# Pooled v summed by GpSimd in all units; batch 0's maxima of v later, and its scale moved to the split of x

## The chip, the cores and the metric

The kernel runs on one core of one Trainium2 chip. The metric is the device time of one execution in microseconds (us). The engines of the core are TensorE (PE, its weight loads PEld), VectorE (DVE), ScalarE (ACT), GpSimd (POOL) and SyncE (SP), which issues all the loads and stores here.

## What is computed

An attention over 8 batches, 8 heads, 576 positions of 64 values, and behind it a gated layer.

```python
q_d = q.reshape(B, H, S // 4, 4, D).mean(axis=3)          # k_d, v_d likewise
out_d = softmax(scale * q_d @ k_d.T) @ v_d                # pooled attention
out_up = np.repeat(out_d, 4, axis=2)
scores = np.where(abs(i - j) < 4, scale * q @ k.T, -1e9)  # local attention
x = out_up + softmax(scores) @ v                          # then (4608, 512)
out = (1 / (1 + exp(-(x @ w_gate))) * (x @ w_val)) @ w_out
```

The gated layer is 512 to 1536 to 512 wide. All inputs are of 32 bits; the products of the layer run as three products of 16-bit halves.

## The kernel before

**Units.** The attention is cut into 32 units: unit u is batch u // 4 and a pair of heads u % 4. Units 0 to 3 are batch 0. A unit's steps are made by unit_steps: prep1 copies q into a block tile; prep2 sums q and k over four positions (sum4, line 383); s0 and s1 are the local scores (tile s, then t), with the row maximum, whose subtraction is GpSimd's; sm sums and scales t; vd (vdsum, line 499) sums v over four positions into vdblk, of which there are two; d0 and d1 are the pooled scores (tile sd), their row maxima mxd and exponentials; dn normalizes them; a0 and a1 transpose t (tile at); v copies v into a block tile; at transposes the pooled weights (tile adt); od (av_down) is the pooled product; x (av_local, xsplit) is the local product, its sum with od in xs, and the split of xs in two 16-bit halves in the tile xT, which the gated layer reads.

**sum4.** Two adds: the first, of 384 or 576 columns, is always GpSimd's; the second (line 387) is GpSimd's too, but for vd it is VectorE's in units 0, 1, 2, 3, 6, 9 and 10 (the list vd). It has two instructions of 64x192, one for each half of the partitions.

**Scales.** Each batch has a scale from the largest |v| of its four units: vmax (line 297) reduces one unit's v on VectorE; in a batch's last unit it takes the maximum over the partitions (max_all, line 121: a transpose on TensorE into the tile mxt, a reduction, a second product) and makes pvb, svb and sxb. sxb is read in batch 0 by the eviction of od (line 568) and by the sum xs (line 584).

**Weights.** They come in 36 tiles of 512 KB, each loaded twice into a ring of five buffers (stage): once for its maximum (hmx, line 154, in max_all for tiles 0 to 3 of gate and value, then for the rest), once for the conversion (wconv, line 201), which has three VectorE instructions a tile and a split. The conversion may overwrite the room that batch 0's inputs lie in, so it begins behind batch 0.

**Banks and order.** The results of TensorE lie in eight banks; two of them (ps_a, "att") serve the local scores, the transposes at and the transposes of the maxima, and the rest serve one name each ("gate", "val", "o0" to "o3"). The tile t has two buffers.

**Order.** Each step is entered with a position (function add), and the steps are traced in the order of positions: batch 0's unit u has its base at 1 + 2.36 u, and a step's offset from the list a_... is multiplied by 0.76. Positions are priorities, not times: a planner at compile time (schedule_with_timeline_sim) draws each engine's queue from them and from its own durations; the engines then work through these queues in order, and a step waits for its data and its buffer. Between the units' steps stand products without use ("awake") in batch 0. From position 56 on (C1) the gated layer of chunks 1 to 8, of 512 rows each, sets the pace, and the units of later batches are placed between its products. Chunk 0 runs beside the conversion of the weights.

Of the kernel before, what the change touches and what calls it, by code (L numbers as in the profile page):

```python
# [12 lines left out]
AF = mybir.ActivationFunctionType  # L13
# [3 lines left out]

T = dict(ma=4.5, mas=0.45, mb=9.5, mbs=0.5, c1=56, gs=2.66, g0=16.84, r1=1.99, rs=1.6, ob=3.16, v0=15.13, v1=16.62, v2=17.5, vs=2.12, o0=18, os=1.2, pro=2.36, u4=13.82, u5=21, u6=27, u7=32, l4=1.3, l5=2.77, l6=9.47, l7=8.68, lv=15.08, vm=1.58, b8=6.75, s8=6.63, b12=26.05, s12=8.17, hold=32.07, al=0.76, am=1, z=3.68, sd=0, sn=0.79, v0m=0.61, xd=[2, 3, 7], ad=[0, 3, 7], aa=[0, 1, 2, 3, 6], td=[0, 3, 9, 10], vd=[0, 1, 2, 3, 6, 9, 10], a_prep1=-2.43, a_prep2=-0.89, a_s0=0.01, a_s1=0.52, a_sm=1.82, a_d0=2.39, a_d1=2.6, a_dn=5.17, a_a0=4.37, a_vd=1.97, a_a1=5.1, a_v=2.74, a_at=5.22, a_od=5.79, a_x=8.38, m_prep0=-3.14, m_prep1=-1.14, m_prep2=-1.43, m_s0=0.69, m_s1=2.59, m_sm=3.12, m_d0=2.84, m_d1=5.8, m_a0=10, m_dn=10.78, m_vd=11.67, m_a1=12, m_v=13.07, m_at=13.44, m_od=15.64, m_x=17, k0=30, k_prep1=4, k_prep2=0, k_s0=2, k_s1=2, k_sm=4, k_d0=3, k_d1=0, k_dn=0, k_a0=3, k_vd=8, k_a1=2, k_v=5, k_at=0, k_od=0, k_x=0)  # L20
P = 128
B, H, S, D = 8, 8, 576, 64
NT = B * S
# [1 line left out]
NPAIR = H // 2  # L25
# [5 lines left out]
SD = S // 4  # L31
# [15 lines left out]
NPLAIN = 8  # L47
# [11 lines left out]
def attention_moe(ctx, tc, qk, qkd, v, vd, wg, wv, wo, mask, out):  # L59
    nc = tc.nc  # L60
# [12 lines left out]
    def awake(n):  # L73
        pt = ps_o.tile([P, 512], F32, tag="val", name="awake")
        for i in range(n):
            nc.tensor.matmul(pt[:, :256], idle[:, :P], idle, start=True, stop=True)

    awake(T["k0"])
    ident = cp.tile([P, P], F32, tag="ident", name="ident")
# [19 lines left out]
    def zeroed(eng, shape, dtype, name):  # L99
        t = cp.tile(shape, dtype, tag=name, name=name)  # L100
        eng.memset(t, 0.0)
        return t
# [10 lines left out]
    ad = zeroed(nc.gpsimd, [QM, 2, NKC, 2, WIN], F32, "ad")  # L113
# [27 lines left out]
    def pow2(dst, src):  # L141

        got = max_all(src, src.shape[1])
        nc.vector.tensor_scalar(out=dst, in0=got, scalar1=TINY, scalar2=None, op0=ALU.max)
        nc.vector.tensor_scalar(
            out=dst.bitcast(I32), in0=dst.bitcast(I32), scalar1=EXPBITS, scalar2=None,
            op0=ALU.bitwise_and)
# [5 lines left out]
    def absmax(dst, src):  # L153
        nc.vector.tensor_reduce(dst, src, axis=AX.X, op=ALU.max, apply_absolute_value=True)  # L154

    def split(hi, lo, src, sc):

        nc.scalar.activation(hi, src, AF.Copy, scale=sc)  # L158
        nc.vector.scalar_tensor_tensor(out=lo, in0=src, scalar=sc, in1=hi, op0=ALU.mult, op1=ALU.subtract)  # L159
# [13 lines left out]
    gs = cp.tile([P, NPC], F32, tag="gs", name="gs")  # L173
# [104 lines left out]
    sxb = cp.tile([P, B], F32, tag="sxb", name="sxb")  # L278
# [16 lines left out]
    vm = {}  # L295

    def vmax(u):
        b, hp = divmod(u, NPAIR)
        if hp == 0:
            vm[b] = wk.tile([P, NPAIR], F32, tag="vm", name=f"vm{b}")  # L300
        absmax(vm[b][:, hp : hp + 1], vraw[u].rearrange("p a b -> p (a b)"))
        if hp == NPAIR - 1:
            m1 = wk.tile([P, 1], F32, tag="vm1", name=f"vm1_{b}")
            nc.vector.tensor_reduce(m1, vm[b], axis=AX.X, op=ALU.max)
            pow2(pvb[:, b : b + 1], m1)
            inv_scaled(svb[:, b : b + 1], pvb[:, b : b + 1], 2.0)
            nc.vector.tensor_scalar(out=sxb[:, b : b + 1], in0=svb[:, b : b + 1], scalar1=4096.0, scalar2=None, op0=ALU.mult)
# [96 lines left out]
    def mine(t, u):  # L404
        assert owner[id(t)] == u, (owner[id(t)], u)
# [7 lines left out]
    def unit_steps(u):  # L413
        b, hp = divmod(u, NPAIR)
        s = st[u] = {}
        NQ = 2 * NJ * R
        plain = u < NPLAIN
# [66 lines left out]
        def p2b():  # L484
# [4 lines left out]
            nc.vector.reciprocal(sm, sm)  # L489
            eng = nc.vector if u in T["td"] else nc.gpsimd  # L490
            eng.tensor_tensor(out=t, in0=t, in1=sm.unsqueeze(2).to_broadcast([P, NBLK, WIN]), op=ALU.mult)  # L491
# [7 lines left out]
        def vdsum():  # L499
            take(VDB)  # L500
            x = vdraw[u].rearrange("p a b f -> p (a b) f")
            sum4([(ps, VDB[ps, :, ps], slice(None)) for ps in HALVES], x, nc.vector if u in T["vd"] else nc.gpsimd)

# [15 lines left out]
        def norm_down():  # L519
# [3 lines left out]
            nc.vector.reciprocal(sme, sme)  # L523
            eng = nc.vector if u in T["ad"] else nc.gpsimd
            for qb in range(2):
                if u in T["aa"]:
                    for h in range(2):
# [34 lines left out]
        def av_down():  # L562
            mine(VDB, u)
            pt = bank("o3", f"od_{u}")
            for c in range(NKC):
                product(pt[:, :SD], [VDB[:, c]], [s["adt"][:, c]], c == 0, c == NKC - 1)
            od = wk.tile([P, SD], F32, tag="od", name=f"od16_{u}")
            nc.scalar.activation(od, pt[:, :SD], AF.Copy, scale=sxb[:, b : b + 1])
            s["od"] = od

        def av_local(i0, i1):
            mine(VT, u)
            pt = bank("gate" if i0 == 0 else "val", f"x_{u}_{i0}")
            for i in range(i0, i1):
                product(pt[:, (i - i0) * R : (i - i0 + 1) * R], [x[:, i] for x in VBp], [x[:, i] for x in s["at"]])
            if i0 == 0:
                s["xs"] = wk.tile([P, S], F32, tag="xs", name=f"xs_{u}", bufs=1)
            t0, t1 = i0 * R, min(i1 * R, S)
            g0, g1 = t0 // 4, t1 // 4
            o = s["xs"][:, t0:t1].rearrange("p (g f) -> p g f", f=4)  # L580
            x = pt[:, : t1 - t0].rearrange("p (g f) -> p g f", f=4)
            y = s["od"][:, g0:g1].unsqueeze(2).to_broadcast([P, g1 - g0, 4])
            if plain:
                nc.vector.scalar_tensor_tensor(out=o, in0=x, scalar=sxb[:, b : b + 1], in1=y, op0=ALU.mult, op1=ALU.add)
            else:
                nc.vector.tensor_tensor(out=o, in0=x, in1=y, op=ALU.add)

        def xsplit():
            for c, o, i, n in segs_of_batch(b):
                x = xtile(c)  # L590
                src = s["xs"][:, i : i + n]
                nc.scalar.copy(x[:, hp, 0, o : o + n], src)  # L592
                eng = nc.vector if u in T["xd"] else nc.gpsimd
                eng.tensor_tensor(out=x[:, hp, 1, o : o + n], in0=src, in1=x[:, hp, 0, o : o + n], op=ALU.subtract)  # L594
            del st[u]
            done.add(u)
# [4 lines left out]
            vd=vdsum, v=plain_v if plain else vsplit,  # L601
            a0=lambda: t_local(0, 3), a1=lambda: t_local(3, 5), at=t_down, od=av_down,
            x=lambda: (av_local(0, 8), av_local(8, 10), xsplit()),
# [68 lines left out]
    def add(pos, f):  # L672
        steps.setdefault(pos, []).append(f)
# [45 lines left out]
    for u in range(NU):  # L719
        b, hp = divmod(u, NPAIR)  # L720
        p0 = base(u)
        for k in ALONE if b == 0 else AMONG:
            add(p0 + offset(u, k), units[u][k])
            if b == 0 and T["k_" + k] and k in ("s0", "s1", "d0", "d1", "a0", "a1", "at", "od", "x"):
                add(p0 + offset(u, k), lambda n=T["k_" + k]: awake(n))
        if b == 0:
            if u == 0:
                add(-10, first_loads)
            add(2 + T["v0m"] * hp, lambda u=u: vmax(u))
            continue  # L730
        if b == 1:
            pl = p0 + offset(u, "prep0") - T[f"l{u}"]
            add(max(pl, base(u - 2) + offset(u - 2, "s1") + 0.1) if u > NPAIR + 1 else pl, lambda u=u: load_qk(u))
            add(T["lv"] + 0.2 * hp, lambda u=u: vload(u))
            after = base(u - 1) + 0.1 if u > NPAIR else 0
            add(max(pl + 0.5, after + offset(u - 1, "prep2") if after else 0), lambda u=u: load_qkd(u))
            add(max(pl + 0.5, after + offset(u - 1, "vd") if after else 0), lambda u=u: load_vd(u))
            add(T["lv"] + T["vm"] * (hp + 1), lambda u=u: vmax(u))
            continue
        add(base(u - 2) - 1 if b > 2 else max(base(u - 2) - 1, T["hold"]), lambda u=u: load_qk(u))  # L740
        add(base(u - 1) - 1 if u > 2 * NPAIR else T["hold"], lambda u=u: load_qkd(u))
        add(base(u - 1) + offset(u - 1, "vd"), lambda u=u: load_vd(u))
        pb = base(b * NPAIR)
        add(pb - 5 + hp, lambda u=u: vload(u))
        add(pb + hp, lambda u=u: vmax(u))
# [116 lines left out]
```

## Time and profile before

| | us |
|---|---|
| median of 3 runs | 1129.31 (1126.57 to 1129.5) |
| profiled execution | 1126.46 |
| its span, first to last instruction | 1124.7 |
| TensorE busy | 1079.2 |
| VectorE busy | 567.7 |
| ScalarE busy | 486.7 |
| GpSimd busy | 356.7 |

The mean granted clock of TensorE is 0.972 of its higher level. The profile is that of one execution: its views give each engine's busy time in a stretch, the chain of work that ended last (followed back from the end, at each step to what released it), the instructions of one engine in order of time with the idle time in front of them, and the instructions of one line or one tile with their durations. A "timeline" row that says x2 stands for two instructions that follow each other.

### The profile page before, as it was taken

What the parts mean: (1) busy time and instruction counts of PE and PEld (TensorE: products, weight loads), DVE (VectorE), ACT (ScalarE), POOL (GpSimd) and SP (SyncE); (2) the same over time, 40 slices, a digit from 0 to 9 for tenths busy, and PEclk for the clock granted to TensorE, in tenths of its full rate; (3) what the DMA queues carried; (4) which work ended last, traced back from release to release, by engine and by line L of the source; (5) the groups of instructions that cost most, each with busy time, mean ns of one, the idle gap of its engine ahead of it and who ended that gap; (6) DMA issues with size and microseconds to landing.
All of it is one profiled execution on the core that took longest, in us unless ns stands there. A gap on an engine that the chain in (4) does not pass through costs nothing.

```text
span 1124.7 us, 15921 instructions
## 1 busy us (share of the span) xinstructions
PE 1079.2 (96%) x6191; PEld 592.0 (53%) x6191; DVE 567.7 (50%) x1050; ACT 486.7 (43%) x1112; POOL 356.7 (32%) x416
## 2 busy tenths in 40 slices
PE   7868878999999999999999999999999999999998
PEld 5753434565555555555555555555555554444443
DVE  7779999854445544444444553544444432112121
ACT  6635666544444444454445443544354332222112
POOL 7435646323323433343333332433243210000000
PEclk8759999999999999999999999999999999999999
DMA  9887766432213222132223121322030000000001
GB/s 368 309 293 276 269 224 197 142 108 80 70 48 126 65 67 70 63 114 71 69 69 108 59 69 56 121 70 66 28 117 14 1 1 38 1 1 38 1 1 38
DMA packets 31899, 110.31 MB, mean 98 GB/s; under 512 B 3536, under 2 KB 3664, under 8 KB 31824
## 3 DMA queue, kind: packets, MB, share of 16 engines
q1 hardware_dynamic: 31824, 109.30, 28.2%
q8 instruction: 49, 0.80, 0.3%
q14 instruction: 26, 0.21, 0.1%
HBM read 99.84 MB, written 9.44 MB: 97 GB/s over the span
## 4 chain that ended last, share of the span: by engine, by line
PE 85%; DVE 8%; ACT 2%; DMA 2%; issue 2%; POOL 1%; DVEq 0%; POOLq 0%; SPq 0%; ACTq 0%
PE po L396 24%; PE pg L396 23%; PE pv L396 23%; PE s L396 5%; PE x L396 3%; PE sd L396 2%; PE od L396 2%; PE at L547 1%; PE adt L557 1%; DVE vdblk L387 1%; DVE hmx L154 1%; DVE wrg L210 1%; DMA wg6c<-in_wg_dram 1%; DVE wrv L209 0%; DVE wrg L209 0%
## 5 line engine op out<-in xcount | busy, mean ns | idle before, releaser
L396 PE MATMUL pg<-xT,wg 128*128 128x512 f16 x1296 | 309.8, 382 | 7.5 <-ACT wg L216 4.3
L396 PE MATMUL pv<-xT,wv 128*128 128x512 f16 x1296 | 310.1, 379 | 3.8 <-DVE tanh L628 3.2
L396 PE MATMUL po<-g,wo 128*128 128x512 f16 x1188 | 280.7, 379 | 0.0
L396 PEld LDWEIGHTS <-wg 128*128 128x128 f16 x1296 | 126.8, 99 | 158.1 <-ACT wg L216 6.9
L396 PEld LDWEIGHTS <-wo 128*128 128x128 f16 x1296 | 126.0, 99 | 149.5 <-ACT wo L158 7.4
L396 PEld LDWEIGHTS <-wv 128*128 128x128 f16 x1296 | 125.5, 98 | 144.0 <-issue 3.1
L628 DVE SCALAR_TENSOR_TENSOR tanh<-tanh,pv 128x512 f32<-128x512 f32 x108 | 73.8, 683 | 195.3 <-PE pv L396 187.6
L620 ACT ACTIVATE tanh<-pg,tsc 128x512 f32<-128x512 f32 (+7 forms) x192 | 86.8, 497 | 153.8 <-PE pg L396 153.3
L636 ACT ACTIVATE g<-tanh,gs 128x512 f16<-128x512 f32 x99 | 71.4, 721 | 149.6 <-DVE tanh L628 148.4
L637 DVE SCALAR_TENSOR_TENSOR g<-tanh,gs,g 128x512 f16<-128x512 f32 x99 | 89.1, 900 | 56.7 <-ACT g L636 56.3
L481 POOL TENSOR_TENSOR t<-t,mx 128x640 f32<-128x640 f32 x32 | 43.9, 1372 | 190.3 <-DVE mx L480 190.3
L396 PEld LDWEIGHTS s<-qk,qblk 128*128 128x128 f32 x600 | 77.0, 196 | 12.3 <-DVE t L469 2.1
L396 PE MATMUL s<-qk,qblk 128*128 128x64 f32 x600 | 76.0, 276 | 4.3 <-DVE t L469 1.5
L594 POOL TENSOR_TENSOR xT<-xs,xT 128x384 f16<-128x384 f32 (+7 forms) x58 | 53.1, 931 | 61.0 <-ACT xT L592 60.2
L491 POOL TENSOR_TENSOR t<-t,sm 128x640 f32<-128x640 f32 x28 | 36.1, 1288 | 89.8 <-DVE sm L489 88.6
L487 DVE TENSOR_REDUCE sm<-t 128x10 f32<-128x640 f32 x32 | 26.1, 817 | 58.3 <-ACT t L482 58.3
L158 ACT ACTIVATE vblk<-v,svb 64x640 f16<-64x640 f32 x48 | 39.6, 825 | 35.4 <-PE x L396 34.0
L440 ACT COPY qblk<-qk 64x580 f32<-64x580 f32 x60 | 40.5, 675 | 24.4 <-DMA qk<-in_qk_dram 17.8
L469 DVE SCALAR_TENSOR_TENSOR t<-s,mk 128x384 f32<-128x384 f32 x64 | 31.1, 486 | 37.6 <-PE s L396 37.4
L513 ACT ACTIVATE mxd<-mxd 72x2 f32<-72x2 f32 x64 | 12.9, 202 | 83.7 <-DVE mxd L512 83.0
L159 DVE SCALAR_TENSOR_TENSOR vblk<-v,svb,vblk 64x640 f16<-64x640 f32 x48 | 46.8, 975 | 4.5 <-ACT vblk L158 2.6
L515 ACT ACTIVATE e<-sd,mxd 72x144 f32<-72x144 f32 x128 | 47.0, 370 | 2.4
(296 smaller groups left out, 1177.7 us busy)
## 6 DMA issues: line engine op xcount, KB each, us to landing
qk<-in_qk_dram SPq DMA_DIRECT2D x30, 610.0 KB, 4.0
qkd<-in_qkd_dram SPq DMA_DIRECT2D x29, 576.0 KB, 3.7
vd<-in_vd_dram SPq DMA_DIRECT2D x29, 384.0 KB, 3.5
v<-in_v_dram SPq DMA_DIRECT2D x32, 320.0 KB, 2.9
out_dram<-osb SPq DMA_DIRECT2D x16, 512.0 KB, 2.9
wo<-in_qk_dram SPq DMA_DIRECT2D x2, 610.0 KB, 9.9
wo<-in_qkd_dram SPq DMA_DIRECT2D x2, 576.0 KB, 9.0
out_dram<-osb SPq DMA_DIRECT2D x4, 256.0 KB, 2.3
```

The costliest lines, as they stand in the source:

```text
L158: nc.scalar.activation(hi, src, AF.Copy, scale=sc)
L159: nc.vector.scalar_tensor_tensor(out=lo, in0=src, scalar=sc, in1=hi, op0=ALU.mult, op1=ALU.subtract)
L396: nc.tensor.matmul(o, w[a], x[c], start=first and i == 0, stop=last and i == len(pairs) - 1)
L440: nc.scalar.copy(QB[ps, :, ps.start : ps.start + R], q_[ps])
L481: nc.gpsimd.tensor_tensor(out=t, in0=t, in1=mx.unsqueeze(2).to_broadcast([P, NBLK, WIN]), op=ALU.subtract)
L491: eng.tensor_tensor(out=t, in0=t, in1=sm.unsqueeze(2).to_broadcast([P, NBLK, WIN]), op=ALU.mult)
L515: nc.scalar.activation(s["e"][:, qb, h, :], pt[:QM, h * SD : (h + 1) * SD], AF.Exp, bias=mx[:, h : h + 1], scale=QKSCALE / 16, accum_out=s ...
L594: eng.tensor_tensor(out=x[:, hp, 1, o : o + n], in0=src, in1=x[:, hp, 0, o : o + n], op=ALU.subtract)
L620: nc.scalar.activation(t[:, o : o + n], pt[:, o : o + n], AF.Tanh, scale=tsc[:, b, fc : fc + 1])
L628: nc.vector.scalar_tensor_tensor(out=t, in0=t, scalar=1.0, in1=pt, op0=ALU.add, op1=ALU.mult)
L636: nc.scalar.activation(g[:, 0], t, AF.Copy, scale=gs[:, fc : fc + 1])
L637: nc.vector.scalar_tensor_tensor(out=g[:, 1], in0=t, scalar=gs[:, fc : fc + 1], in1=g[:, 0], op0=ALU.mult, op1=ALU.subtract)
```

## The change

It does four things.

- The list vd is empty: the second add of the pooled v is GpSimd's in all units. In batch 0 the step vd moves from offset 1.97 to 2.6, so behind d0 (2.39) and, at the same position, behind d1 (2.6).
- vmax of batch 0's units stands at 5.5 + 0.3 for each unit in place of 2 + 0.61 for each.
- In batch 0 od is evicted without the scale, and xs is a plain sum.
- In batch 0 the split of x applies the scale: ScalarE makes the high half of scale times xs, and VectorE the low half in one operation of three operands (split, line 156). Before, a copy made the high half and a subtraction the low one: on GpSimd in units 0 and 1, on VectorE in units 2 and 3 (the list xd).

```diff
-T = dict(..., v0m=0.61, ..., vd=[0, 1, 2, 3, 6, 9, 10], ..., a_vd=1.97, ...)
+T = dict(..., v0m=0.61, ..., vd=[], ..., a_vd=2.6, ...)
...
             od = wk.tile([P, SD], F32, tag="od", name=f"od16_{u}")
-            nc.scalar.activation(od, pt[:, :SD], AF.Copy, scale=sxb[:, b : b + 1])
+            if u < NPAIR:
+                nc.scalar.copy(od, pt[:, :SD])
+            else:
+                nc.scalar.activation(od, pt[:, :SD], AF.Copy, scale=sxb[:, b : b + 1])
...
-            if plain:
+            if NPAIR <= u < NPLAIN:
                 nc.vector.scalar_tensor_tensor(out=o, in0=x, scalar=sxb[:, b : b + 1], in1=y, op0=ALU.mult, op1=ALU.add)
             else:
                 nc.vector.tensor_tensor(out=o, in0=x, in1=y, op=ALU.add)
...
                 src = s["xs"][:, i : i + n]
+                if u < NPAIR:
+                    split(x[:, hp, 0, o : o + n], x[:, hp, 1, o : o + n], src, sxb[:, b : b + 1])
+                    continue
                 nc.scalar.copy(x[:, hp, 0, o : o + n], src)
...
-            add(2 + T["v0m"] * hp, lambda u=u: vmax(u))
+            add(5.5 + 0.3 * hp, lambda u=u: vmax(u))
```

## Rows read from the trace of the kernel before

**Rows 1.** The page, busy time of TensorE: us, share of the span, instructions.
```profile
PE 1079.2 (96%) x6191; PEld 592.0 (53%) x6191; DVE 567.7 (50%) x1050; ACT 486.7 (43%) x1112; POOL 356.7 (32%) x416
```

**Rows 2.** Busy time by stretch: length, engines' us (instructions), granted clock, DMA share, GB/s.
```profile
20.00:40.00 20.00, 14.43 (x68) 12.79 (x68) 14.20 (x34) 11.24 (x39) 8.52 (x11) 0.62 1.03 407
...
60.00:80.00 20.00, 13.78 (x60) 12.30 (x59) 14.24 (x29) 4.49 (x10) 3.77 (x7) 0.50 0.79 278
...
160.00:200.00 40.00, 31.39 (x148) 16.28 (x149) 37.48 (x62) 26.12 (x56) 22.23 (x16) 0.90 0.64 203
200.00:250.00 50.00, 50.00 (x278) 28.62 (x276) 37.29 (x69) 24.20 (x51) 15.49 (x16) 0.98 0.32 114
```

**Rows 3.** Chain of waits, 8 to 45 us: shares; then start us, us, what.
```profile
by line: DVE vdblk L387 21.5%; PE s L396 16.7%; issue 10.7%; PE x L396 6.6%; DVE mxd L512 5.1%; PE od L396 4.9%; DVE vm L154 4.4%; DVE mx L480 4.2%; PE sd L396 4.0%; ACT e L515 3.6%; POOL t L481 3.4%; DVE t L469 3.3%; PE awake L76 3.0%; ACT
...
11.96 0.92 DVE vdblk L387
12.89 1.38 DVE vdblk L387
...
42.38 0.88 DVE vdblk L387
43.27 1.04 DVE vdblk L387
```

**Rows 4.** TensorE's timeline, 0 to 95 us: start, us, engine, line, operation, tiles, idle.
```profile
23.29 1.81 PE L396 MATMUL od<-adt,vdblk 128*128 128x144 f32 x6 [2.28 <-ACT adt L539]
...
30.14 0.27 PE L127 MATMUL mxt<-ident,vm 128*1 128x128 f32 x1 [2.40 <-DVE vm L304]
30.25 0.49 PE L547 MATMUL at<-ident,t 128*128 128x128 f32 x3
...
34.57 4.46 PE L396 MATMUL s<-wo,qblk 128*128 128x64 f32 x20
...
52.71 0.27 PE L127 MATMUL mxt<-ident,hmx 128*8 128x128 f32 x1
52.82 1.45 PE L396 MATMUL s<-wo,qblk 128*128 128x64 f32 x12
```

**Rows 5.** VectorE's timeline, 0 to 135 us.
```profile
18.21 1.86 DVE L491 TENSOR_TENSOR t<-t,sm 128x640 f32<-128x640 f32 x1
...
29.07 0.82 DVE L154 TENSOR_REDUCE vm<-v 128x1 f32<-128x640 f32 x1
...
32.84 0.14 DVE L307 TENSOR_SCALAR sxb<-svb 128x1 f32<-128x1 f32 x1
...
39.07 0.42 DVE L469 SCALAR_TENSOR_TENSOR t<-s,mk 128x256 f32<-128x256 f32 x1 [0.56 <-PE s L396]
...
50.94 0.68 DVE L154 TENSOR_REDUCE hmx<-wv3m 128x1 f32<-128x512 f32 x1
...
64.19 0.69 DVE L594 TENSOR_TENSOR xT<-xs,xT 128x512 f16<-128x512 f32 x1
...
127.04 1.44 DVE L387 TENSOR_TENSOR vdblk<-vd 64x192 f32<-64x192 f32 x2
```

**Rows 6.** GpSimd's timeline, 0 to 110 us.
```profile
21.71 1.22 POOL L387 TENSOR_TENSOR kdblk<-wo 64x144 f32<-64x144 f32 x2
...
48.83 1.12 POOL L387 TENSOR_TENSOR vdblk<-vd 64x192 f32<-64x192 f32 x2 [0.26 <-PE od L396]
```

**Rows 7.** Line 387 by engine: count, ns min/median/max, first and last start us, shape.
```profile
L387 POOL TENSOR_TENSOR vdblk<-vd x50: 515/526/1629, 48.8 to 871.4; 64x192 f32<-64x192 f32 x50
...
L387 DVE TENSOR_TENSOR vdblk<-vd x8: 502/587/1378, 12.0 to 274.2; 64x192 f32<-64x192 f32 x8
...
L387 DVE TENSOR_TENSOR vdblk<-wv x4: 877/1036/1043, 26.5 to 43.3; 64x192 f32<-64x192 f32 x4
```

**Rows 8.** The tile wv3m: issue by SyncE's queue, and us to landing.
```profile
L184 SPq DMA_DIRECT2D wv3m<-in_wv_dram x1: 328/328/328, 33.6 to 33.6; - x1
...
DMA to landing us min/median/max: 8.5/8.5/8.5
```

More of the change, by code (lines that the diff above doesn't have):

```diff
@@ L16 @@
 PSUM = bass.MemoryType.PSUM
-T = dict(ma=4.5, mas=0.45, mb=9.5, mbs=0.5, c1=56, gs=2.66, g0=16.84, r1=1.99, rs=1.6, ob=3.16, v0=15.13, v1=16.62, v2=17.5, vs=2.12, o0=18, os=1.2, pro=2.36, u4=13.82, u5=21, u6=27, u7=32, l4=1.3, l5=2.77, l6=9.47, l7=8.68, lv=15.08, vm=1.58, b8=6.75, s8=6.63, b12=26.05, s12=8.17, hold=32.07, al=0.76, am=1, z=3.68, sd=0, sn=0.79, v0m=0.61, xd=[2, 3, 7], ad=[0, 3, 7], aa=[0, 1, 2, 3, 6], td=[0, 3, 9, 10], vd=[0, 1, 2, 3, 6, 9, 10], a_prep1=-2.43, a_prep2=-0.89, a_s0=0.01, a_s1=0.52, a_sm=1.82, a_d0=2.39, a_d1=2.6, a_dn=5.17, a_a0=4.37, a_vd=1.97, a_a1=5.1, a_v=2.74, a_at=5.22, a_od=5.79, a_x=8.38, m_prep0=-3.14, m_prep1=-1.14, m_prep2=-1.43, m_s0=0.69, m_s1=2.59, m_sm=3.12, m_d0=2.84, m_d1=5.8, m_a0=10, m_dn=10.78, m_vd=11.67, m_a1=12, m_v=13.07, m_at=13.44, m_od=15.64, m_x=17, k0=30, k_prep1=4, k_prep2=0, k_s0=2, k_s1=2, k_sm=4, k_d0=3, k_d1=0, k_dn=0, k_a0=3, k_vd=8, k_a1=2, k_v=5, k_at=0, k_od=0, k_x=0)
+T = dict(ma=4.5, mas=0.45, mb=9.5, mbs=0.5, c1=56, gs=2.66, g0=16.84, r1=1.99, rs=1.6, ob=3.16, v0=15.13, v1=16.62, v2=17.5, vs=2.12, o0=18, os=1.2, pro=2.36, u4=13.82, u5=21, u6=27, u7=32, l4=1.3, l5=2.77, l6=9.47, l7=8.68, lv=15.08, vm=1.58, b8=6.75, s8=6.63, b12=26.05, s12=8.17, hold=32.07, al=0.76, am=1, z=3.68, sd=0, sn=0.79, v0m=0.61, xd=[2, 3, 7], ad=[0, 3, 7], aa=[0, 1, 2, 3, 6], td=[0, 3, 9, 10], vd=[], a_prep1=-2.43, a_prep2=-0.89, a_s0=0.01, a_s1=0.52, a_sm=1.82, a_d0=2.39, a_d1=2.6, a_dn=5.17, a_a0=4.37, a_vd=2.6, a_a1=5.1, a_v=2.74, a_at=5.22, a_od=5.79, a_x=8.38, m_prep0=-3.14, m_prep1=-1.14, m_prep2=-1.43, m_s0=0.69, m_s1=2.59, m_sm=3.12, m_d0=2.84, m_d1=5.8, m_a0=10, m_dn=10.78, m_vd=11.67, m_a1=12, m_v=13.07, m_at=13.44, m_od=15.64, m_x=17, k0=30, k_prep1=4, k_prep2=0, k_s0=2, k_s1=2, k_sm=4, k_d0=3, k_d1=0, k_dn=0, k_a0=3, k_vd=8, k_a1=2, k_v=5, k_at=0, k_od=0, k_x=0)
 P = 128
```

## The prediction

> **What bounds the kernel now.** I read the page's busy times first: TensorE is busy for 96% of the span [rows 1]. That is a mean over two different stages, so the next view is the busy time by stretch [rows 2]. From 200 us on TensorE is busy without a gap, 50.00 of 50 us (the row of 200 to 250 stands for those behind it, down to the last few us): nothing that GpSimd, VectorE or ScalarE save there can be seen. Between 160 and 200 us it is busy for 31.39 of 40 us and VectorE for 37.48: there VectorE, which converts the weights, is the bound. Between 20 and 80 us no engine is full (VectorE 14.20 of 20 us, then again 14.24) and the granted clock falls to 0.62 and 0.50: here a chain of waits through all engines sets the pace. This is the stage of units 0 to 3 (batch 0). So the end of the kernel moves with two things: the length of that chain, and VectorE's work up to 200 us. TensorE's work after 200 us isn't touched.
>
> The chain of waits between 8 and 45 us comes next [rows 3]. The reader is to see its largest share: 21.5% of 37 us, 7.95 us, are the second adds of the pooled v on VectorE (L387), two for each of four units; unit 0's pair and unit 3's stand there with 2.30 and 1.92 us. An add of 64x192 takes 502 ns at least on VectorE and about 1.04 us in the middle of this stage, and 526 ns at the median on GpSimd [rows 7].
>
> Then TensorE's queue [rows 4]. After od of unit 0 and what follows it, it stands at mxt, the transpose that batch 0's maxima need, for 2.40 us until VectorE has the last maximum (30.14 us), and only then takes the transposes at of unit 0 (30.25 us). Their input was scaled on VectorE at 18.21 us for 1.86 us, so ready at 20.1 us [rows 5]: they stood some ten us for another reason. Both use the two banks "att", and every use of these banks runs in the program's order: scores of unit 0, of unit 1, mxt, at of unit 0, scores of unit 2. The same is seen at 52.71 us: the transpose of the weights' maxima, and directly behind it the scores of unit 3 (52.82 us). The scores of unit 2 (34.57 us) wait for at of unit 0 twice over, for the bank and because the score tile has two buffers.
>
> **The change part by part.**
> - Adds off VectorE, batch 0: minus 8 instructions, 7.95 us on the chain [rows 3]. What is late next? Behind each pair stands a maximum of the down-sampled scores (mxd), whose scores are then long there; for units 0 and 1 all of it is gained until the next floor, GpSimd.
> - Adds onto GpSimd: 8 times 0.526 is 4.2 us [rows 7]. GpSimd's other queue entries are the sums of q and k for the next unit, the subtraction of the row maximum, and the scaling of t. The step vd moves behind d0 and d1 and behind the next unit's sum of q and k, so those are held up by less. The bound: kdblk of unit 2 ends at 21.71 plus 1.22, 22.9 us [rows 6], and its reader comes behind od of unit 0, which ends at 25.1 us [rows 4]; slack 2.2 us. Two units' adds are ahead of it, 2.1 us: hidden if nothing else moves, but the reader wants it sooner by what the earlier pairs gave up (2.30 us for the first). On the path between 0 and 4.2 us; I take 1.5, near the row that shows the slack. New waits: unit 2's add writes the tile that od of unit 0 reads, unit 3's that of unit 1; behind them on GpSimd stand the scaling of t and the next sums. Unit 4's add, on GpSimd already, ran in 1.12 us for the pair [rows 6].
> - GpSimd's price shows no penalty here: 526 ns against 502 to 587 on VectorE [rows 7]. The Trainium skill (GPSIMD Engine Reference, Engine selection) says that an elementwise operation of two inputs is about twice as slow there; by that the eight adds would be about 8.0 us, an estimate from twice the 502 ns, and the sum would lose some 2 us of its gain. The rows decide, and do not agree with the rule for this shape.
> - Maxima later (5.5 to 6.4 in place of 2 to 3.83): the same 8 operations. What moves is the order of the banks: at of unit 0 and the scores of unit 2 now stand ahead of mxt, at of unit 1 behind it. At of unit 0 no longer waits for the last maximum (29.07 us) and its transpose; the scores of unit 2 can start once at and x of unit 0 are done, which takes from 30.25 to 34.57 us, 4.3 us. Od of unit 0 ends at 25.1 us now, and 2 to 4 us sooner without the early pairs: an estimate of 25 to 28 us for these scores. That overlaps with the adds (the chain through unit 2's pair ends in the same place), so I count nothing on its own and keep up to 2.5 us for the low end.
> - od unscaled, x added without the scale: od of unit 0 waited for the scale (sxb, 32.84 us [rows 5]); now its bank is free after od, and od of unit 1 can follow. Same instructions, 0 us by themselves.
> - Split with the scale: ScalarE scales in place of copying, 0. VectorE takes the low half of units 0 and 1 from GpSimd: a 512-wide one takes 0.69 us [rows 5], with its 64-wide rest about 0.8 a unit, 1.6 in all. Whether the three-operand form costs as much no row of this shape shows; between 0 (idle VectorE hides it) and 2.1 us for all four units. I take half of the 1.6, plus 0.8.
> - Unit 6: minus 1.44 us of VectorE at 127 us, in its full stretch [rows 5], against about 1.1 us on GpSimd, which is busy for only 22.23 of 40 us at 160 to 200 us [rows 2]; minus 1.0, between 0 and 1.4. Units 9 and 10 lie behind 200 us, 0 us.
>
> What limits the gain behind that: the scores of unit 3 stand behind the weights' transpose, whose last maximum ran at 50.94 us [rows 5], while its load was issued at 33.6 us and landed 8.5 us later, at 42.1 [rows 8]. VectorE was late there by 8.8 us, so a gain of 6 to 8 us still passes.
>
> Sum: -7.95 + 1.5 + 0.8 - 1.0 = -6.65 us. From the profiled 1126.46 us (span 1124.7) that gives 1119.8. The runs shown are 1126.57, 1129.31 and 1129.5; with the profiled one their mean is 1128.0, 1.5 above it. I forecast 1121 us.
>
> **The rivals.**
> 1. The gain is absorbed. The order of every queue is drawn by a planner at compile time, from its own costs of loads. If it still lets the weights' maxima wait, the scores of unit 3 come at 52.8 us as now and the 8 us become idle time on VectorE; only unit 6 is left, 1 us, and the split takes 0.8 back: 1128. For it: VectorE stands idle for 5.8 of 20 us at 20 to 40 us [rows 2]; against: that idle lies behind the adds and mxt. Chance 0.20.
> 2. Slower: the maxima meet the chain. Four reductions of 0.82 us and the run from the last of them to the scale (29.07 to 33.0 us, 3.9 us [rows 5]) lie now where the chain waits for others. The planner may put them behind t of unit 2 (39.07 us), in the dense stretch, with at of unit 1 behind mxt: 3.3 + 3.9, less unit 3's pair 1.92, plus 1.6 for the split. That is 6.9, less the 1.0 of unit 6: 1128.0 + 5.9 = 1134. It decides if the scores of unit 2 do not come well before 34.57 us: then the early adds' gain is lost. For it: the new positions are behind those of unit 2's scores by the numbers; against: VectorE is idle for 5.8 us at 20 to 40 us [rows 2], more than the four reductions take. Chance 0.15.
> 3. Better: the scores of unit 2 come at 26 us, and the stretch of 60 to 80 us, where TensorE is busy for 13.78 us at a granted clock of 0.50 [rows 2], the lower of its two levels (1.2 GHz in place of 2.4), gets the higher one for most of it; up to 2.5 us and 5 of the 6.9 that this would halve away, 1113 to 1114. Chance 0.15.
> 4. It doesn't do what it says: the adds run on GpSimd, but VectorE is slowed elsewhere by as much, since adds on VectorE differ between 502 and 1378 ns with what runs beside them [rows 7]. This ends like rival 1 and is in its chance.
>
> **How the numbers follow.** The forecast, 1116 to 1125, has 0.50. The range that holds 8 in 10 reaches from better (1112) to absorbed and a little beyond (1132). A measurement of this kernel can tell some 0.3%, 3.4 us, from no change: faster, below 1126, is the forecast and the better case, 0.65; within, 0.20; slower 0.15.
>
> **What would show it.** Right: no L387 on VectorE; the chain of waits before 45 us without it; at of unit 0 and the scores of unit 2 ahead of mxt in TensorE's queue, the scores before 29 us; the first gate product some 6 us sooner; VectorE's stretch over 37 of 40 us ends 6 us sooner. Wrong: mxt or GpSimd's adds on the chain; scores of unit 3 at 52 us as before; GpSimd waiting for od with t behind it. The forecast would fail above all if the planner's new order of VectorE, not the work in it, sets when the weights' conversion begins.

## The result

| | before | changed |
|---|---|---|
| median, us | 1127.94 (1125.39 to 1129.5) | 1117.38 (1115.59 to 1118.06) |
| profiled execution, us | 1126.46 | 1115.59 |
| its span, us | 1124.7 | 1113.8 |

The ratio of the changed kernel to the one before is 0.9904, with a 95% interval of 0.9879 to 0.9928: 10.8 us faster (8.1 to 13.6). The forecast was 1121 us, so the way was right, the gain of some 7 us was too small by a third, and the time lies inside 1112 to 1132.

The page's busy times, to be read against [rows 1]:

```profile
PE 1074.3 (96%) x6191; PEld 588.9 (53%) x6191; DVE 556.9 (50%) x1040; ACT 487.5 (44%) x1112; POOL 369.3 (33%) x426
```

TensorE is busy for as large a share as before, so the 10.9 us of span are 6.0 us of idle time (45.5 to 39.5) and 4.9 us of busy time, for the same 6191 products (the mean granted clock went from 0.972 to 0.980). VectorE has 10.8 us less, GpSimd 12.6 us more. By stretch, against [rows 2] (length, busy us of PE, PEld, DVE, ACT and POOL, granted clock, DMA share, GB/s):

```profile
20.00:40.00 20.00, 16.53 (x129) 13.79 (x127) 16.01 (x42) 19.00 (x61) 14.31 (x21) 1.00 1.03 406
40.00:60.00 20.00, 14.02 (x60) 12.34 (x60) 15.46 (x37) 6.80 (x15) 7.62 (x12) 0.53 0.90 345
60.00:80.00 20.00, 17.55 (x73) 12.63 (x73) 17.05 (x31) 9.92 (x22) 5.45 (x5) 0.62 0.94 342
...
160.00:200.00 40.00, 33.86 (x171) 17.30 (x170) 38.95 (x62) 27.00 (x54) 24.20 (x18) 0.96 0.65 221
200.00:250.00 50.00, 50.00 (x285) 29.59 (x284) 30.27 (x58) 19.69 (x43) 15.64 (x20) 1.00 0.27 88
```

Between 20 and 40 us the granted clock is now 1.00 in place of 0.62, and TensorE does 129 products in place of 68. Between 40 and 60 us it is the other way round: 0.53 in place of 0.84, and 60 products in place of 119. From 200 us on TensorE is full, as before. Between 160 and 200 us VectorE is fuller than it was, 38.95 of 40 us.

The chain of waits of 8 to 45 us, against [rows 3]:

```profile
by line: DMA qk<-in_qk_dram 21.4%; ACT ad L528 14.8%; ACT e L515 11.9%; ACT qblk L440 9.5%; PE sd L396 6.6%; issue 5.6%; ACT t L482 5.4%; DVE xT L159 5.3%; PE adt L557 5.3%; PE od L396 4.2%; DVE vm L154 3.9%; ACT wg L446 3.6%; ACT xT L158 3
...
37.97 1.98 DVE xT L159 x2
39.95 1.46 DVE vm L154 x2
```

Line 387 is gone from the shares, where it had 21.5%. The chain now starts at a load of q and k (7.93 us, of which 3.1 lie in this window) and then goes mostly through ScalarE: the five of its lines that the list shows whole have 45%. Between 20 and 40 us ScalarE is busy for 19.00 of 20 us, 11.24 before [rows 2]; no term of the forecast had it, and no run below shortens its work. New are also the low half of unit 1's split at 37.97 us and, behind it, the maxima of the next batch on VectorE. TensorE's queue, against [rows 4]:

```profile
17.97 0.75 PE L547 MATMUL at<-ident,t 128*128 128x128 f32 x5
...
20.49 1.45 PE L396 MATMUL s<-wo,qblk 128*128 128x64 f32 x12
...
27.83 0.27 PE L127 MATMUL mxt<-ident,vm 128*1 128x128 f32 x1
...
42.78 0.38 PE L557 MATMUL adt<-ident,ad 72*128 72x72 f32 x1 [5.22 <-ACT ad L528]
...
46.52 0.42 PE L127 MATMUL mxt<-ident,hmx 128*8 128x128 f32 x1
46.74 2.66 PE L396 MATMUL s<-wo,qblk 128*128 128x64 f32 x12
...
72.27 1.06 PE L396 MATMUL pg<-xT,wg 128*128 128x512 f16 x2
```

The order of the two banks is the one that was read off the numbers of the positions: the transposes at of unit 0 first (17.97 us), then the scores of unit 2 (20.49 us, 14.1 us sooner than before), and only then mxt (27.83 us). Behind that TensorE stands for 5.22 us at 42.78 us, and the scores of unit 3, again directly behind the transpose of the weights' maxima, come at 46.74 us, 6.1 us sooner. The first gate product is at 72.27 us, 9.2 us sooner than in the kernel before:

```profile
81.43 1.03 PE L396 MATMUL pg<-xT,wg 128*128 128x512 f16 x2 [3.43 <-ACT wg L216]
```

VectorE's timeline, against [rows 5]:

```profile
17.07 0.82 DVE L491 TENSOR_TENSOR t<-t,sm 128x640 f32<-128x640 f32 x1
...
25.31 0.81 DVE L154 TENSOR_REDUCE vm<-v 128x1 f32<-128x640 f32 x1
...
31.80 0.15 DVE L307 TENSOR_SCALAR sxb<-svb 128x1 f32<-128x1 f32 x1
...
32.93 0.95 DVE L159 SCALAR_TENSOR_TENSOR xT<-xs,sxb,xT 128x512 f16<-128x512 f32 x2 [0.39 <-ACT xT L158]
...
37.97 1.98 DVE L159 SCALAR_TENSOR_TENSOR xT<-xs,sxb,xT 128x512 f16<-128x512 f32 x2 [1.17 <-ACT xT L158]
...
43.45 0.68 DVE L154 TENSOR_REDUCE hmx<-wv2m 128x1 f32<-128x512 f32 x1
...
44.64 0.68 DVE L154 TENSOR_REDUCE hmx<-wv3m 128x1 f32<-128x512 f32 x1
```

The last maximum of v is read at 25.31 us, 3.8 us sooner; sxb follows at 31.80 us, and only the split waits for it (its low half at 32.93 us). The maxima of the weights wv2m and wv3m are taken at 43.45 and 44.64 us (wv3m at 50.94 before). GpSimd, against [rows 6] and [rows 7]:

```profile
17.09 1.21 POOL L387 TENSOR_TENSOR vdblk<-wo 64x192 f32<-64x192 f32 x1
...
22.49 0.97 POOL L387 TENSOR_TENSOR kdblk<-wo 64x144 f32<-64x144 f32 x2
...
25.87 1.13 POOL L387 TENSOR_TENSOR vdblk<-wv 64x192 f32<-64x192 f32 x2
```

```profile
L387 POOL TENSOR_TENSOR vdblk<-vd x58: 518/527/977, 12.6 to 860.5; 64x192 f32<-64x192 f32 x58
...
L387 POOL TENSOR_TENSOR vdblk<-wv x4: 528/530/534, 25.9 to 31.1; 64x192 f32<-64x192 f32 x4
```

Unit 2's kdblk ends at 23.5 us, 0.5 us later than before. Seven of batch 0's eight adds cost 0.53 us each on GpSimd, the two of unit 2 together 1.13 us; one of unit 1 took 1.21 us (17.09 us).

The loads tell where the middle of the stage had stood. The rate of all loads between 40 and 60 us, in GB/s, one number for each half us; first the kernel before:

```profile
GB/s 410 418 401 410 393 246 171 304 285 51 0 0 0 33 0 0 166 341 396 212 65 25 106 270 344 434 393 430 260 375 371 254 383 426 385 410 385 393 254 123
```

Then the changed kernel:

```profile
GB/s 418 393 410 410 410 401 427 404 400 419 398 402 392 409 431 393 397 418 410 418 401 401 426 401 401 270 164 49 25 8 66 147 270 360 401 434 361 322 383 350
```

Before, the loads came nearly to rest at 45 to 48 us: all five buffers of the ring held weights that had landed (the fifth at 44.6 us) and waited for VectorE to take their maxima (the first at 49.29 us). In the changed kernel the loads run on at some 400 GB/s until 52 us.

### The profile page after: what moved, and what is told of

It reads as the page before. It is cut to its first block, busy times and chain, and to the rows that moved or that the text cites. A ratio compares the mean times of both kernels' runs of the same rounds, so it can differ in the third digit from the quotient of the medians.

```text
span 1113.8 us, 15920 instructions
## 1 busy us (share of the span) xinstructions
PE 1074.3 (96%) x6191; PEld 588.9 (53%) x6191; DVE 556.9 (50%) x1040; ACT 487.5 (44%) x1112; POOL 369.3 (33%) x426
## 4 chain that ended last, share of the span: by engine, by line
PE 85%; DVE 7%; DMA 3%; ACT 3%; issue 1%; POOL 1%; SPq 0%; DVEq 0%; ACTq 0%; POOLq 0%
PE po L396 24%; PE pv L396 23%; PE pg L396 23%; PE s L396 5%; PE x L396 3%; PE sd L396 2%; PE od L396 2%; PE at L547 1%; PE adt L557 1%; DMA qkd<-in_qkd_dram 1%; DMA qk<-in_qk_dram 1%; DVE wrg L209 1%; DVE wrv L209 1%; ACT qblk L440 1%; POOL qkd L385 1%
## 5 line engine op out<-in xcount | busy, mean ns | idle before, releaser
L600 POOL TENSOR_TENSOR xT<-xs,xT 128x384 f16<-128x384 f32 (+7 forms) x54 | 49.7, 933 | 50.8 <-ACT xT L598 49.8
L589 DVE TENSOR_TENSOR xs<-x,od 128x464 f32<-128x464 f32 (+1 forms) x56 | 23.5, 451 | 50.2 <-PE x L396 45.9
```

## Where the time ends: one mark in all the kernels

The conversion of the value weights ends with one instruction of line 210 on wv11c. First the kernel before, then the changed one:

```profile
192.14 0.68 DVE L210 SCALAR_TENSOR_TENSOR wrv<-wv11c,wrv 128x512 int32<-128x512 int32 x1
...
181.93 0.63 DVE L210 SCALAR_TENSOR_TENSOR wrv<-wv11c,wrv 128x512 int32<-128x512 int32 x1
```

From it to the end of the span are 932.6 and 931.9 us. This holds for the kernels below too: 930.3 to 933.8 us in all but awake_more (937.7). So the question "where did the time go" has a place: VectorE's busy and idle time up to that mark. The rows are VectorE's busy time up to it (length; busy us and instructions; granted clock, DMA share, GB/s), for the kernel before:

```profile
0.00:192.14 192.14, 167.34 (x320) 0.86 0.77 277
```

and for the changed kernel:

```profile
0.00:181.93 181.93, 158.90 (x313) 0.89 0.82 293
```

Before, 167.3 us of work and 24.8 us of idle time; changed, 158.9 and 23.0. The mark came 10.2 us sooner by 8.4 us less work and 1.8 us less idle time. Whether work that is taken away turns into idle time is what the parts below differ in.

| kernel | VectorE's work, us | its idle time, us | mark at, us | median, us | ratio to before (95%) |
|---|---|---|---|---|---|
| before | 167.3 | 24.8 | 192.1 | 1127.94 | |
| changed | 158.9 | 23.0 | 181.9 | 1117.38 | 0.9904 (0.9879 to 0.9928) |
| adds_alone | 157.0 | 38.5 | 195.5 | 1126.82 | 0.9983 (0.9964 to 1.0002) |
| all_but_adds | 168.5 | 22.7 | 191.2 | 1124.72 | 0.9964 (0.9945 to 0.9982) |
| unscaled_alone | 169.3 | 23.7 | 193.0 | 1130.14 | 1.0019 (1.0009 to 1.0030) |
| later_adds_back | 161.1 | 22.8 | 183.9 | 1117.56 | 0.9906 (0.9891 to 0.9921) |
| adds_early_step | 161.1 | 22.7 | 183.7 | 1117.67 | 0.9912 (0.9893 to 0.9932) |
| adds_twice | 154.7 | 32.3 | 187.0 | 1122.34 | 0.9955 (0.9940 to 0.9970) |
| weight_scales_late | 158.5 | 28.1 | 186.6 | 1120.98 | 0.9945 (0.9930 to 0.9960) |
| before_weight_scales_late | 170.2 | 22.4 | 192.6 | 1126.40 | 0.9990 (0.9977 to 1.0002) |
| awake_more | 161.4 | 24.5 | 185.9 | 1125.07 | 0.9981 (0.9969 to 0.9992) |
| half_loads | 163.7 | 23.9 | 187.6 | 1120.78 | 0.9940 (0.9920 to 0.9960) |
| half_loads_scales_late | 160.6 | 19.6 | 180.3 | 1116.30 | 0.9905 (0.9886 to 0.9924) |
| half_loads_before | 168.3 | 24.4 | 192.7 | 1123.84 | 0.9968 (0.9953 to 0.9983) |

Work, idle time and mark are those of one profiled execution each, the medians and ratios those of the timed runs. An execution can lie some 2.5 us off its kernel's median: the changed kernel's profiled one was its fastest (1115.59 us), the one before lies 1.5 us below its median, that of all_but_adds 1.8 and that of half_loads_before 2.5 us above. So differences of 3 us between two marks say little. The ratios compare with runs of the kernel before that were made beside each kernel (medians 1127.17 to 1128.03 us); gains over the kernel before are worked out from them and differ by up to a microsecond from the differences of the medians shown.

## The experiments

Two theories stood against each other at first: A, that the order of the two banks makes the gain, and B, that the adds off VectorE make it.

**adds_alone.** The kernel before with

```diff
-vd=[0, 1, 2, 3, 6, 9, 10], a_vd=1.97
+vd=[], a_vd=2.6
```

> The kernel before with the pooled v summed by GpSimd everywhere and its step at 2.6; maxima, od and split as before. Theory A (the order of the two banks makes the gain: the transpose for the maxima no longer stands ahead of unit 0's transposes): that transpose still stands ahead, only the VectorE chain up to it gets shorter by 2 to 6 us, so unit 2's scores start at 29 to 32 us (34.57 before, 20.49 in the changed kernel) and the time is 1123 to 1126. Theory B (the 8 adds off VectorE make the gain): 1119 or less, near the changed kernel's 1117.4.

Measured: 1126.82 us, 1.9 us faster (4.1 faster to 0.2 slower). TensorE's queue:

```profile
26.39 0.42 PE L127 MATMUL mxt<-ident,vm 128*1 128x128 f32 x1
...
32.74 4.48 PE L396 MATMUL s<-wo,qblk 128*128 128x64 f32 x20
...
54.42 0.42 PE L127 MATMUL mxt<-ident,hmx 128*8 128x128 f32 x1
54.63 2.66 PE L396 MATMUL s<-wo,qblk 128*128 128x64 f32 x12
```

The scores of unit 2 come at 32.74 us, 1.8 us sooner, since mxt still stands ahead of unit 0's transposes; the scores of unit 3 even come later (54.63 us). B falls. A's own range (1123 to 1126) was missed by 0.8 us too: not even the 2 us arrive with certainty. VectorE's row up to the mark shows where the work went:

```profile
0.00:195.46 195.46, 156.96 (x310) 0.83 0.78 273
```

10.4 us less work than before, and 13.7 us more idle time (195.5 - 157.0 = 38.5). The work was on the chain of waits, and yet taking it away gave next to nothing: the next release came hardly sooner. (Some 2 of the 13.7 us are spread: the two profiled executions lie 0.8 us above and 1.5 us below their kernels' medians.)

**all_but_adds.** The changed kernel with

```diff
-vd=[], a_vd=2.6
+vd=[0, 1, 2, 3, 6, 9, 10], a_vd=1.97
```

> The changed kernel with the adds of units 0 to 3, 6, 9 and 10 back on VectorE and their step at 1.97. Theory A: unit 2's scores still start before 27 us, the adds cost the chain 2 to 5 us again: 1119 to 1122. Theory B: 1125 to 1128, as before the change.

Measured: 1124.72 us, 4.1 us faster than before (2.0 to 6.2), between the two theories' ranges, so outside both. TensorE's queue and two rows of VectorE:

```profile
20.43 0.76 PE L547 MATMUL at<-ident,t 128*128 128x128 f32 x5 [1.15 <-DVE t L491]
...
21.98 1.55 PE L396 MATMUL s<-wo,qblk 128*128 128x64 f32 x12 [0.47 <-ACT at L539]
...
52.60 0.38 PE L127 MATMUL mxt<-ident,hmx 128*8 128x128 f32 x1 [2.65 <-DVE hmx L154]
52.77 2.66 PE L396 MATMUL s<-wo,qblk 128*128 128x64 f32 x12
```

```profile
47.48 2.49 DVE L159 SCALAR_TENSOR_TENSOR xT<-xs,sxb,xT 128x512 f16<-128x512 f32 x2 [1.39 <-ACT xT L158]
...
51.87 0.67 DVE L154 TENSOR_REDUCE hmx<-wv3m 128x1 f32<-128x512 f32 x1
```

The order of the banks does what A says: the scores of unit 2 at 21.98 us. But those of unit 3 are at 52.77 us, where they were before: the weights' maxima end at 51.87 + 0.67 us. Ahead of them in VectorE's queue stand the adds and the low half of unit 1's split, at 47.48 us and 2.49 us long. Up to the mark:

```profile
0.00:191.16 191.16, 168.50 (x323) 0.83 0.79 279
```

2.1 us less idle time, but 1.2 us more work. So the two halves of the change are worth 1.9 and 4.1 us, and 10.8 together: 4.8 us exist only with both (some 0.7 to 8.9 us, an estimate from the three intervals put together). Without the order the freed VectorE time stands idle; without the free time VectorE is late for what the order lets through. The granted clock between 20 and 40 us goes with the order: 0.62 before, 0.61 in adds_alone, 0.91 here and 1.00 in the changed kernel. No run holds it apart, so what part of the order's gain is the clock's stays open.

**unscaled_alone.** The kernel before with od unscaled and the scale in the split: the change's edits of av_down, av_local and xsplit alone. The list vd, the step's place and the maxima's place stay as they were.

> The kernel before with od unscaled and the scale in the split, the maxima at their old place, the adds on VectorE. Theory A: the transpose for the maxima still stands ahead of unit 0's transposes, unit 2's scores start at 33 to 35 us, and VectorE has 1.6 us more: 1127 to 1130. A rival, that the freed bank of od makes the gain: od of unit 1 before 36 us (40.52 before) and 1122 or less.

Measured: 1130.14 us, 2.1 us slower (1.0 to 3.4). Mxt stands ahead, as before, and unit 2's scores come later than before:

```profile
30.20 0.27 PE L127 MATMUL mxt<-ident,vm 128*1 128x128 f32 x1 [1.53 <-DVE vm L304]
...
36.25 4.46 PE L396 MATMUL s<-wo,qblk 128*128 128x64 f32 x20
```

Od of unit 1 came at 31.66 us, 8.9 us sooner (40.52 before), as the rival wanted, and the time got longer: the freed bank brings nothing of its own. VectorE has 2.0 us more work up to the mark, and the time shows it. The later place of the maxima can't be tried without the unscaled od: od of unit 0 would read a scale that isn't made yet. That part alone is open.

**later_adds_back.** The changed kernel with `vd=[6, 9, 10]`.

> The changed kernel with the adds of units 6, 9 and 10 back on VectorE. If unit 6's 1.44 us lie in VectorE's full stretch as forecast: 1 to 1.5 us slower than the changed kernel, 1118.4 to 1119. If nothing of it is on the path: 1117.4 within 0.8. If the planner's order matters more than the work: off by 2 us or more either way.

Measured: 1117.56 us, 0.2 us more than the changed kernel. The work of unit 6 is back (161.1 in place of 158.9 us to the mark), but in the medians nothing of it is seen; the profiled span is 2.1 us longer against the changed kernel's fastest execution.

**adds_early_step.** The changed kernel with `a_vd=1.97`.

> The changed kernel with the step of the pooled v of batch 0 at its old place (1.97 in place of 2.6), ahead of the next unit's sum of q and k on GpSimd. If the forecast's slack on GpSimd (2.2 us ahead of unit 2's pooled scores) is right: unit 2's scores still start before 23 us and the time is within 2 us of the changed kernel, 1116 to 1119.5. If the adds ahead of those sums hold the pooled scores up: 1120 or more.

Measured: 1117.67 us, unit 2's scores at 20.16 us. The place of the step is worth nothing that can be told.

**adds_twice.** The changed kernel with the second adds of units 0 to 3 done twice on GpSimd (vdsum passes u < NPAIR as twice):

```diff
-    def sum4(out, x, eng=nc.gpsimd):
+    def sum4(out, x, eng=nc.gpsimd, twice=False):
...
-        for ps, o, g in out:
-            eng.tensor_tensor(out=o, in0=x[ps, g, 0], in1=x[ps, g, 1], op=ALU.add)
+        for i in range(2 if twice else 1):
+            for ps, o, g in out:
+                eng.tensor_tensor(out=o, in0=x[ps, g, 0], in1=x[ps, g, 1], op=ALU.add)
```

> The changed kernel with the second adds of v of units 0 to 3 done twice on GpSimd, 8 instructions of 0.53 us more. If GpSimd's adds are hidden: within 1 us of the changed kernel (1117.4). If they lie on the path as the forecast's 1.5 us: 1 to 2 us slower. If all of it does: 4 us and more. What goes beyond 4.2 us either way is the planner's new order.

Measured: 1122.34 us, 5.0 us slower than the changed kernel for 4.2 us of work. GpSimd's queue:

```profile
35.54 2.37 POOL L388 TENSOR_TENSOR vdblk<-wv 64x192 f32<-64x192 f32 x4 [1.83 <-PE od L397]
...
45.03 1.26 POOL L492 TENSOR_TENSOR t<-t,sm 128x640 f32<-128x640 f32 x1 [3.88 <-ACT adt L540]
```

The adds at 35.54 us wait 1.83 us for od of unit 1, and the scaling of unit 2's t comes at 45.03 us (36.66 in the changed kernel). VectorE's idle time grows by 9.3 us, and its work falls by 4.2. So more adds are not hidden here. That GpSimd has no slack at all isn't shown: it stood idle for 5.02 us ahead of 36.66 us in the changed kernel, and how much of the 5.0 us is the planner's new order this run doesn't separate.

**weight_scales_late.** The changed kernel with the weights' first transposes as a step of its own behind unit 2's:

```diff
-            if k == "v" and i == b - 1:
+            if k == "v" and i == b - 1 and a > 0:
...
+    def first_scales():
...
+        scales_of(0, 4)
...
+    add(10.2, first_scales)
```

> The changed kernel with the first transposes of the weights' maxima and the scales behind them as a step of their own at 10.2, behind the transposes of unit 2 and ahead of those of unit 3, not ahead of unit 3's scores. If the banks' order is what holds unit 3's scores (46.74 us in the changed kernel): they start before 36 us, x of unit 2 before 48 (54.02) and the time falls by 3 to 8 us, to 1109 to 1114. If VectorE's work, not the chain, decides from there on: within 2 us of the changed kernel.

Measured: 1120.98 us, 3.6 us slower than the changed kernel and outside both ranges. TensorE's queue:

```profile
31.87 1.51 PE L396 MATMUL s<-wo,qblk 128*128 128x64 f32 x12
...
71.27 1.03 PE L396 MATMUL pg<-xT,wg 128*128 128x512 f16 x2 [8.28 <-ACT wg L216]
```

The scores of unit 3 come at 31.87 us, 15 us sooner, and batch 0 is through at 57.7 us; behind the scores of the next unit TensorE then waits 8.28 us for the first converted weight. The order of the banks is no longer what holds the end. VectorE's idle time to the mark is 28.1 us, 5.1 more.

**before_weight_scales_late.** The same edit in the kernel before.

> The same edit in the kernel before. If unit 3's scores behind the weights' transposes are what swallows the gain of either half of the change: unit 3's scores at 45 to 47 us in place of 52.82, behind unit 1's transposes, and 1121 to 1125. If the batch's own maxima hold the chain more: 1126 to 1129, as before.

Measured: 1126.40 us, 1.1 us faster (2.6 faster to 0.2 slower); the scores of unit 3 at 45.78 us, the mark at 192.6 us. The place in the chain moved by 7 us and the end hardly.

**awake_more.** The changed kernel with more products without use, to see what the granted clock costs:

```diff
+            if u == 3 and k == "d1":
+                add(p0 + offset(u, k), lambda: awake(36))
+            if u == 2 and k == "x":
+                add(p0 + offset(u, k), lambda: awake(24))
```

> The changed kernel with 36 more products without use behind unit 3's pooled scores and 24 behind unit 2's local product, where TensorE stood for 5.2 and 3.7 us. If the granted clock of 0.53 at 40 to 60 us and 0.62 at 60 to 80 costs what the products take longer (some 2 us for x of unit 2 and 2 to 4 for the scores and x of unit 3): the clock is above 0.8 there and the time 1112 to 1115. If TensorE's pace is not on the path there: 1117 within 1.5.

Measured: 1125.07 us, 7.7 us slower. The clock rose to 0.88 between 60 and 80 us, but only from 0.53 to 0.61 between 40 and 60:

```profile
60.00:80.00 20.00, 15.40 (x88) 9.30 (x86) 17.36 (x31) 9.46 (x20) 5.65 (x5) 0.88 0.91 319
```

and 12 products of x of unit 3 took 1.55 us in place of 2.81, but began at nearly the same time (63.37 us; 63.69 in the changed kernel):

```profile
63.37 1.55 PE L396 MATMUL x<-at,wg 128*128 128x58 f32 x12 [0.32 <-ACT at L539]
```

Between 60 and 80 us the clock was not on the path: unit 3's last local product ended 3.2 us sooner (66.70 against 69.91 us), but the first gate product began only 0.7 us sooner (71.61 us) and waited 2.87 us for a converted weight. The mark is at 185.9 us, 4.0 later, and the end 5.8 us further behind it than in the changed kernel. Why that is so isn't settled: the planner draws all later queues anew, and no run takes the two apart.

A third theory, C, came from the loads' rates: that from 40 us on the stream of loads decides when the conversion begins. Three kernels load only half of each tile in the first pass and reduce it twice. VectorE's time doesn't quite stay by that: a half takes 0.40 us, so two take 0.80 in place of 0.68.

```diff
+        n = WPC if why == "c" else WPC // 2
-        last_w[0] = nc.sync.dma_start(t.rearrange("p a b -> p (a b)"), srcs[k][i].bitcast(I32))
+        last_w[0] = nc.sync.dma_start(t[:, :n].rearrange("p a b -> p (a b)"), srcs[k][i][:, :n].bitcast(I32))
...
-        absmax(o, t[:, :, 1].bitcast(F32))
+        for _ in range(2):
+            absmax(o, t[:, : WPC // 2, 1].bitcast(F32))
```

**half_loads**, in the changed kernel:

> The changed kernel with the first pass over the weights loading half of each tile (256 KB for 512) and reducing that half twice, so that VectorE's time for it stays (two of about 0.34 us for one of 0.67). The maxima are those of half the columns: part of the computation is left out. Theory C (from 40 us on the stream of weight loads through its ring of five buffers decides when the conversion begins): the first conversion on VectorE (67.6 us in the changed kernel) begins at or before 64 us and the time is 1108 to 1114. If the chain of units 2 and 3 decides: conversion at 66 to 68 us, 1116 to 1119.

Measured: 1120.78 us, 3.4 us slower. The first conversion on VectorE began at 59.77 us, 6.2 us sooner than in the changed kernel, as C says (the 67.6 us of the expectation are the third instruction on that tile). First the changed kernel, then half_loads:

```profile
65.95 0.43 DVE L208 TENSOR_SCALAR wrg<-wg0c 128x512 int32<-128x512 int32 x1 [1.28 <-ACT wg0c L207]
...
59.77 0.41 DVE L210 TENSOR_SCALAR wrg<-wg0c 128x512 int32<-128x512 int32 x1
```

But the first gate product came later, and VectorE was busy for 19.61 of 20 us between 60 and 80 us (17.05 in the changed kernel):

```profile
75.67 3.73 PE L398 MATMUL pg<-xT,wg 128*128 128x512 f16 x9
```

**half_loads_scales_late**, in weight_scales_late:

> The same half loads with the weights' scales as a late step, where unit 3 was done at 57.7 us and TensorE stood 8.28 us for the first converted weight (first gate product at 71.27 us, 1121.0). Part of the computation is left out as in the other. Theory C: first gate product at 60 to 64 us and 1110 to 1114. If the loads are not what it stood for: 70 us or later and 1119 to 1122.

Measured: 1116.30 us, 4.7 us faster than weight_scales_late; its expected range was lower.

```profile
65.41 1.06 PE L398 MATMUL pg<-xT,wg 128*128 128x512 f16 x2
```

Here the 8.28 us wait was for the loads: the first gate product is 5.9 us sooner.

**half_loads_before**, in the kernel before:

> The kernel before with the same half loads, so with part of the computation left out. Theory C: its DMA queues stood idle at 45 to 50 us, since the ring waited for VectorE and not VectorE for the ring, so bytes are not its limit there: less gain than in the changed kernel, 1122 to 1128. If bytes are the limit in both: 6 us or more faster than before, under 1122.

Measured: 1123.84 us, 3.6 us faster than before (1.9 to 5.3). The first conversion began at 65.0 us, 11.6 us sooner than the 76.56 us before, and the mark is at 192.7 us, where it was, in an execution 2.5 us slower than the median. The expected range was hit, but not its reason: "less gain than in the changed kernel", where there was none.

C falls as a cause by itself. The start of the conversion moved by 6.2 and 11.6 us, and VectorE's idle time up to the mark stayed within 1 us (23.9 against 23.0, 24.4 against 24.8). It fell only where batch 0 is out of the way: 19.6 against 28.1 us in half_loads_scales_late. The price of the loads in time isn't clean, since the halves add work (4.8 us to the mark in half_loads); and where half_loads_before has its 3.6 us from, no trace shows.

## Why the prediction was right, point by point

- **What bounds the kernel.** Right in the main. From 200 us on TensorE is full in both, and 10.2 of the 10.9 us stand ahead of the mark. The next floor that the forecast named behind the adds was GpSimd; in the changed kernel the chain runs mostly through ScalarE, which had no term.
- **Adds off VectorE, 7.95 us.** The term was mis-sized as a gain of its own. They were on the chain of waits as read [rows 3], and VectorE's work fell by 10.4 us in adds_alone, more than the adds themselves; the measured gain alone is 1.9 us. The chain of waits says what was late, not what comes next; here it was mxt in front of unit 0's transposes. Behind the new order the same adds are worth 6.7 us (4.1 to 10.8), near the 7.45 that the forecast's three terms for them make (7.95 - 1.5 + 1.0).
- **Order of the banks, counted at nothing on its own with up to 2.5 us kept.** The mechanism was read rightly from [rows 4], down to the order of the three steps; unit 2's scores came at 20.49 us, sooner than the 25 to 28 us of the estimate. Its size was wrong: all_but_adds is worth 4.1 us, with the cost of the split inside it. The forecast's sum put one half at its full price and the other at zero; both are needed. With both, VectorE's work to the mark is 8.4 us less and no idle time takes its place. That the forecast still came within 4 us is in part luck: one term too large, when taken alone, and one too small made up for each other.
- **GpSimd, 1.5 us out of 0 to 4.2.** Kdblk of unit 2 slipped by 0.5 us and was read 3.1 us after its end (the pooled scores at 26.53 us), so the slack was real there. Adds_twice shows that more is not hidden: another 4.2 us cost 5.0, with a new order in it. The 1.5 us themselves no run shows. Seven of the eight adds took 0.53 us as in [rows 7], one 1.21. The Trainium skill's factor of two for an operation of two inputs (GPSIMD Engine Reference, Engine selection) doesn't appear for this shape, 527 ns at the median; the forecast went by the rows, and rightly.
- **Split with the scale, 0.8 us.** Too small by what the runs show: with od unscaled it costs 2.1 us alone (1.0 to 3.4), and its low half stands in the chain of the changed kernel at 37.97 us.
- **Unit 6, 1.0 us.** Not there: 0.2 us in later_adds_back, inside what can be told.
- **The limit at unit 3's scores.** The forecast let a gain of 6 to 8 us pass there; 6.1 us did. The rest was won behind it: the first gate product is 9.2 us sooner (some 6 forecast) and the first conversion on VectorE 10.6 (65.95 in place of 76.56 us), with the loads no longer at rest. But half_loads and half_loads_before moved that start by 6.2 and 11.6 us without a like gain, so which later step carries the rest isn't shown.
- **Rivals.** Absorbed (0.20): this is what the adds do by themselves. The maxima meeting the chain (0.15): they didn't, unit 2's scores came in time, by the point that the forecast named. Better (0.15): the clock rose between 20 and 40 us, and at 60 to 80 only from 0.50 to 0.62; in awake_more it was 0.88 there, and the kernel was slower.

## What to carry to other kernels

When a chain of waits names one engine's work, look for the next release behind it before that work is counted as a gain: work that is taken away becomes idle time unless the next thing in line can start. Two edits of which each gives little can be worth more together, so try them as a pair, and add up one engine's work and idle time to a fixed mark to see which of the two an edit changed. Where results share banks that are taken in the program's order, as the two here, a late reduction in front of ready work costs more than its own time.

## What the runs showed of the hardware

Two instructions of line 159 (512 and 64 wide, both inputs in SBUF, where the tiles lie) took 0.95 us at 32.93 us and 1.98 us at 37.97 us on VectorE. At 32.93 us GpSimd stood idle (30.52 + 1.12 us to 36.66 us); at 37.97 us it worked almost without a gap from 36.66 us on. The same is in [rows 7], 502 ns at least and 1036 ns at the median in batch 0's stage for one add. It goes both ways, and the one that starts second pays: VectorE's scaling of t took 0.82 us at 17.07 us, and GpSimd's add that began 0.02 us behind it took 1.21 in place of 0.53; in the kernel before, the same scaling began 0.08 us behind a GpSimd instruction of 1.26 us (18.13 us) and took 1.86 [rows 5]. The Trainium skill (SBUF — State Buffer, Who interferes with whom) says that a VectorE instruction with two inputs in SBUF contends with a GpSimd instruction that reads SBUF, and that issue order decides who blocks; these durations agree. So an add that leaves VectorE for GpSimd also makes GpSimd busier beside the VectorE instructions that stay.
